# A recurrent-memory attention layer with a gated MLP on one core: everything but the AV products in 32-column TensorE tiles, both AV products side by side in shared accumulators, side work in one accumulator

## The chip, the core and the metric

The kernel runs on one core of a Trainium2 chip. The metric is the device time of one launch in microseconds. TensorE (PE; its weight loads are listed apart as PEld), VectorE (DVE), ScalarE (ACT), GpSimd (POOL) and SyncE (SP, which issues the DMAs here) each run their own instruction queue in order and meet at semaphores.

## What is computed

The reference, cut to what matters. S = 2048 tokens, Dm = 512, H = 32 heads of Dh = 128, M = 8 memory rows, segments of 32 tokens (64 of them).

```python
mem = mem0
for s in range(n_seg):
    h = concat([mem, x[s*32:(s+1)*32]])              # 40 rows
    q, k, v = h @ Wq, h @ Wk, h @ Wv                 # per head
    scores = where(mask, q @ k.T * scale, -1e9)
    p = softmax(scores)
    o = (p @ v) @ Wo
    mem = o[:8]                                      # goes into the next segment
    outs.append(o[8:])
a = concat(outs)
b = gelu(layernorm(x) @ w1 + b1) @ w2 + b2
g = sigmoid((x * gate_w).sum(-1))
out = g * a + (1 - g) * b
```

The memory rows make the 64 segments a strict recurrence: the first matmul of a segment needs the last result of the segment before.

## The kernel before

**Stages.** A first stage computes the MLP branch and the gate for all tokens, and ends at about 104.7 us. Then one Python loop, `for s in range(nseg + 2)`, unrolls the 64 segments; a *tile* is four segments (`T, si = divmod(s, 4)`, 128 tokens). The order of every engine's instructions is that of the program text (a manual schedule).

**Rows.** Of a segment's 40 rows, 32 (8 memory, 24 tokens) ride through the loop body in `hT`; the remaining 8 tokens of each of a tile's four segments, the "left" rows, are computed for a whole tile at once, one tile ahead, as side work.

**One segment, in the order of PE's queue.** (1) Q and K in five accumulators, four 32-column tiles side by side (`qk_unit`); each is transposed in 32x32 blocks by DVE from PSUM into an fp32 tile `Tt` (`qk_tr`) and cast to bf16 into `QT` or `KT` by ACT, one of them by POOL. (2) The first half of V, cast by ACT. (3) `scores`, added in PSUM bank 7 to a mask that `mask_mm` wrote there in the segment before; in between and after them the second half of V. (4) ACT's `Exp`, first over the 16 columns of the memory queries, then over the rest, into `E`. (5) `sm`, the sums for the memory queries: two matmuls with the block matrix `BO`; DVE's reciprocal `R`, and DVE's product `Pm`. (6) The AV product of the memory rows, `Um`, in 32-row tiles (`av`). (7) `sr`, the sums for the token queries, in bank 7, and DVE's reciprocal of them, 256 columns long. (8) DVE and ACT cast `Um` into `UTT`. (9) Wo in two halves of 256 columns (`wo_unit`) for the new memory rows and the token rows of two segments before; casts into `wsb`. (10) `mask_mm` for the next segment in bank 7. (11) The AV product of the token rows of segment s-1 (`av_x`), from `Px`, which POOL multiplied (`x_mul`) once the long reciprocal was there. (12) Four small matmuls of `wsb` with `Sel`, which write the transposed new memory into bank 7, and DVE's cast into the next `hT`. `ux_out`, at the head of the next segment, lets ACT cast the token rows' AV product into `UTT`.

**Side work.** `side_work(T, si)` is a generator; each `next` issues one unit, four matmuls of 512 columns side by side. For si = 0 it gives 8 units of V of the left rows (`left_v`), for si = 1 and 2 8 units of their Q and K (`left_qk`), for si = 3 2 units of `out_units` and 8 of `wo_left`. `run_fill(n)` places n units: 5 behind `sm` (6 for si = 3), 1 behind `sr`, 2 ahead of (12) for si = 3; what is left follows (12). Tiles 0 and 15 have no side units in some of their segments. A unit's accumulator comes from `side`, banks 5 and 6 in turn; its evictions wait in two lists, `dve_q` and `act_q`, which `flush` empties at fixed places, and earlier if `side` needs the bank.

**Left Q and K.** DVE transposes the accumulator as in (1) into `Tt`, and POOL casts from there into `QL` and `KL`.

**Banks.** Q, K, V and the AV products rotate through banks 0 to 4 (`ring`); 7 holds mask, scores, `sr` and the new memory in one tile, so that `mask_mm` waits for whoever read the last one there.

```python
            S_next = mask_mm()
        if live and s >= 1:
            av_x(s - 1, (ne, na, nc_, nb))
        run_fill(2 * (si == 3))
```

Of the kernel before, what the change touches and what calls it, by code (L numbers as in the profile page):

```python
# [23 lines left out]
def kernel(ctx, tc, A_x, A_mem0, A_Wq, A_Wk, A_Wv, A_Wo, A_seg_len, B_x, B_w1, B_b1, B_w2, B_b2, gate_w, out):  # L24
    nc = tc.nc
    P = 128
# [147 lines left out]

    pools.update(nTt=2, nside=1)

# [13 lines left out]
    def later(q, ev, k):  # L190
        side_todo.add(k)
        q.append((k, ev))

    def side(shape, dtype=FP32):
        side_n[0] += 1
        n = pools["nside"]
        while side_n[0] - n in side_todo:
            flush(dve_q)
            flush(act_q)
        return bank(5 + side_n[0] % n, shape, dtype)  # L200

# [51 lines left out]
    def left_qk(T, t, hf):  # L253
        h0, h1 = HF[hf]
        bk = side([P, 512])
        side_k = side_n[0]
        for kc in range(KC):
            qk_unit(bk, GLs[T], t, h0, h1, kc)
            if kc < KC - 1:
                yield  # L260
        def ev():
            Tv = qk_tr(bk, h0, h1)
            if t == 0:
                nc.gpsimd.tensor_copy(out=QL[T % 2][:, h0:h1, :], in_=Tv)
            else:
                for hh in range(h0 // 8, h1 // 8):
                    r0 = 8 * hh - h0
                    nc.gpsimd.tensor_copy(out=KL[T % 2][:, :, :, hh, :], in_=Tv[:, r0:r0 + 8, :].rearrange("p g (s c) -> p g s c", c=LEFT))
        later(dve_q, ev, side_k)
        yield  # L270

    def left_v(T, vb):
        bk = side([P, 512])
        side_k = side_n[0]
        for kc in range(KC):
            v_unit(bk, GLs[T], vb, kc)
            if kc < KC - 1:
                yield

        def ev():  # L280
            vt = pools["sb"].tile([P, 4, Dh], BF16, tag="vt", bufs=1, name="vt")
# [12 lines left out]

        later(act_q, ev, side_k)
        yield
# [19 lines left out]
    def out_units(T):  # L316
        ob = side([P, Dm])
        side_k = side_n[0]
# [8 lines left out]
        def ev():  # L327
            o_sb = cw.tile([P, Dm], BF16, tag="o", bufs=1, name="o")
            nc.vector.scalar_tensor_tensor(out=o_sb[:], in0=ob[:], scalar=g_all[:, T:T + 1], in1=c_all[:, T, :], op0=ALU.mult, op1=ALU.add)
            nc.sync.dma_start(out2[T * P:(T + 1) * P, :], o_sb[:])  # L330
        later(dve_q, ev, side_k)
        yield
# [19 lines left out]
    def prep_q(s):  # L352
        T, si = divmod(s, SPT)
        nc.gpsimd.tensor_copy(out=QT[:, :, 32:40], in_=QL[T % 2][:, :, LEFT * si:LEFT * si + LEFT])

    def mask_mm():

        B = bank(7, [P, 512])
        S = B[:, 0:NG * EW].rearrange("p (i e) -> p i e", e=EW)
        nc.tensor.matmul(S, lhsT=ident[:], rhs=MkA[:].unsqueeze(2).to_broadcast([P, 4, 2, EW]),  # L360
                         start=True, stop=True, skip_group_check=True)
        return B, S
# [14 lines left out]

    def av(U, n, s, V, Pt, c_main, c_left, u0):

        T, si = divmod(s, SPT)  # L380
        for i in range(NG):
            for j in range(4):
                q = slice(32 * j, 32 * j + 32)
                nc.tensor.matmul(U[j][:, i, :], lhsT=V[q, i, :], rhs=Pt[q, i, c_main:c_main + n],  # L384
                                 start=(i == 0), stop=False, skip_group_check=True, tile_position=(32 * j, 0))
        for g in range(2):
# [97 lines left out]
    def setup():  # L484
# [13 lines left out]
        for hf in range(2):  # L498
            for t in range(2):
                yield from left_qk(0, t, hf)  # L500
                flush(dve_q)
                yield
        left_v_in(0)
# [75 lines left out]
    cw = loop.enter_context(tc.tile_pool(name="cw", bufs=2))  # L579
    pools.update(ps=pb, sb=cw, nTt=3, nside=2)  # L580

# [24 lines left out]

    def av_x(s, banks):
        U = [bank(k, [P, NG, 32]) for k in banks]
        av(U, 32, s, Vs.pop(s), Pxs.pop(s), 0, 32, 24)
        Uxs[s] = U  # L610

    def ux_out(s):
        T, si = divmod(s, SPT)
        c0 = 24 - 8 * si
        for j, U in enumerate(Uxs.pop(s)):
            nc.scalar.copy(out=UTT[T % 2][:, :, j, c0 + M:c0 + 40], in_=U[:])  # L616

    for s in range(nseg + 2):
# [11 lines left out]
        if live:  # L630
            B, S = S_next
            na, nb, nc_, nd, ne = ring
            ring = (nd, ne, na, nc_, nb)
            qk_banks = (na, nb, nc_, nd, ne)
# [27 lines left out]
            for kc in range(1, KC):  # L662
# [6 lines left out]
            sm = bank(nc_, [P, NG, 8])  # L669
            nc.tensor.matmul(sm[:], lhsT=BO[:], rhs=E[:, :, 8:16], start=True, stop=False)  # L670
            nc.tensor.matmul(sm[:], lhsT=BO[:], rhs=E[:, :, 0:8], start=False, stop=True)  # L671
            nc.scalar.copy(out=v_out(V, 1), in_=vb1[:])
            run_fill(5 + (si == 3))
            nc.vector.reciprocal(out=R[:, 0:8 * NG].rearrange("p (i q) -> p i q", q=8), in_=sm[:])  # L674
            Pm = cw.tile([P, NG, 16], BF16, tag="Pm", bufs=1, name="Pm")
            nc.vector.tensor_tensor(out=Pm[:].rearrange("p i (a q) -> p i a q", q=8), in0=E[:, :, 0:16].rearrange("p i (a q) -> p i a q", q=8),  # L676
                                    in1=R[:, 0:8 * NG].rearrange("p (i q) -> p i q", q=8).unsqueeze(2).to_broadcast([P, NG, 2, 8]), op=ALU.mult)
            Um = [bank(k, [P, NG, 8]) for k in (nd, ne, na, nc_)]
            av(Um, 8, s, V, Pm, 8, 0, 0)
            sr = B[:, 0:NG * 32].rearrange("p (i q) -> p i q", q=32)  # L680
            nc.tensor.matmul(sr, lhsT=BO[:], rhs=E[:, :, 16:48], start=True, stop=False, skip_group_check=True)  # L681
            nc.tensor.matmul(sr[:, :, 24:32], lhsT=BO[:], rhs=E[:, :, 48:56], start=False, stop=True, skip_group_check=True)
            Tp, sp = divmod(s - 2, SPT)
            for j in range(4):
                (nc.scalar.copy if j % 2 else nc.vector.tensor_copy)(out=UTT[Tp % 2][:, :, j, 24 - 8 * sp:24 - 8 * sp + M], in_=Um[j][:])  # L685
            nc.vector.reciprocal(out=R[:, 8 * NG:].rearrange("p (i q) -> p i q", q=32), in_=sr)  # L686
            run_fill(1)
        else:
            if s == nseg:
                ux_out(s - 2)  # L690
                x_mul(s - 1)
                av_x(s - 1, (ne, na, nc_, 7))
            else:
                ux_out(s - 2)
# [3 lines left out]
        for half in range(2):  # L698
            d = slice(256 * half, 256 * half + 256)
            wp = bank((nb, nd)[half], [P, 256])  # L700
            for u in range(8):
                wo_unit(wp, UTT[Tp % 2], 24 - 8 * sp, u, 256 * half, 256 * half + 256)
            if half == 0:
                flush(act_q, 2)
            (nc.scalar.copy if half else nc.vector.tensor_copy)(out=wsb[:, d], in_=wp[:])  # L705
        if s >= 2:
            wsbs[s] = wsb
        if s + 1 < nseg:
            S_next = mask_mm()
        if live and s >= 1:  # L710
            av_x(s - 1, (ne, na, nc_, nb))
        run_fill(2 * (si == 3))
        if s + 1 < nseg:
            aT = S_next[0][:, NG * EW:NG * EW + KC * M].rearrange("p (k m) -> p k m", m=M)
            for m in range(KC):
                nc.tensor.matmul(aT[:, m, :], lhsT=wsb[:, m * P:(m + 1) * P], rhs=Sel[:, 0:M], start=False, stop=True, skip_group_check=True)  # L716
            nc.vector.tensor_copy(out=hn[:, :, 0:M], in_=aT)  # L717
# [3 lines left out]
    for _ in out_units(NT - 2):  # L721
        flush(dve_q, 9)
    for _ in wo_left(NT - 1):
# [138 lines left out]
```

## Time and profile before

| | us |
|---|---|
| median of 6 runs | 838.56 (838.32 to 839.36) |
| the profiled execution: its time | 839.98 |
| its span | 838.1 |
| PE busy | 809.0 (97%) |
| DVE busy | 502.5 (60%) |
| ACT busy | 434.3 (52%) |
| POOL busy | 274.6 (33%) |
| a segment with si = 0, 1, 2 / 3 (a tile from 509.78) | 11.00, 10.95, 11.04 / 11.66 |

The loop of 64 segments takes from 104.7 us to the end, and nearly all of them have the length of the last row, so a segment is the unit to think in: 0.1 us of a segment is about 6.4 us of the whole. A segment begins where PE starts the first matmul on the new `hT`.

In timelines a line is a group of like instructions that follow each other on one engine: start, time from the first one's start to the last one's end, engine, line of the kernel, operation, tiles. Matmuls are pipelined, so the end of one group lies behind the start of the next. The form `128*32` is a weight tile of 128 rows and 32 columns; `128*128` takes the whole array, `32*128` is a 32-row tile.

### The profile page before, as it was taken

The numbers are of one execution on the slowest core, as the hardware profiler recorded it, in microseconds if no ns is written. First come the engines' busy times: TensorE is split into PE (matmuls) and PEld (weight loads), VectorE is DVE, ScalarE is ACT, GpSimd is POOL, SyncE is SP. The second block draws the span as 40 slices with busy tenths as digits, with TensorE's granted clock in tenths as the row PEclk, the third lists the DMA queues.
The fourth block names the chain that finished last, engine by engine and source line by source line (L and its number), as shares of the span: only waits on it lengthen the run. The fifth ranks groups of instructions, "written<-read, shape, count | busy, mean of one in ns | idle before, by whom it ended". The sixth has DMA issues, their size and how long they took to land.

```text
span 838.1 us, 49253 instructions
## 1 busy us (share of the span) xinstructions
PE 809.0 (97%) x22417; PEld 494.0 (59%) x22417; DVE 502.5 (60%) x1019; ACT 434.3 (52%) x1245; POOL 274.6 (33%) x625
## 2 busy tenths in 40 slices
PE   6999999999999999999999999999999999999886
PEld 3665455666666556665665665666556656665553
DVE  5763156565656666665666565666666565656553
ACT  3554445545554555545555545455554555455552
POOL 8000134242433243243424242433333243424220
PEclk9999999999999999999999999999999999999999
DMA  9790300000000010101010100001010101010000
GB/s 312 262 384 26 102 26 13 25 15 15 25 19 27 10 36 10 36 11 34 5 31 15 30 17 21 25 18 28 10 36 10 36 10 36 4 35 6 10 5 23
DMA packets 38216, 37.64 MB, mean 45 GB/s; under 512 B 13545, under 2 KB 36434, under 8 KB 36466
## 3 DMA queue, kind: packets, MB, share of 16 engines
q1 hardware_dynamic: 37874, 34.31, 12.4%
q8 instruction: 177, 2.90, 1.5%
q14 instruction: 37, 0.30, 0.1%
q0 software_dynamic: 128, 0.13, 0.1%
HBM read 26.03 MB, written 6.29 MB: 39 GB/s over the span
## 4 chain that ended last, share of the span: by engine, by line
PE 93%; DVE 3%; DMA 1%; issue 1%; SPq 1%; ACT 1%; DVEq 0%; ACTq 0%
PE b L211 34%; PE b L233 17%; PE b L222 17%; PE b L384 5%; PE hp L456 4%; PE bp L473 4%; PE b L360 2%; PE b L369 2%; PE b L681 2%; PE b L716 1%; PE b L389 1%; PE b L670 1%; DMA Wo_sb<-in_A_x_dram 1%; PE b L320 1%; PE b L373 0%
## 5 line engine op out<-in xcount | busy, mean ns | idle before, releaser
L217 DVE STREAM_TRANSPOSE Tt<-b 128x512 f32<-128x512 f32 (+1 forms) x384 | 225.9, 614 | 86.9 <-PE b L211 72.7
L211 PEld LDWEIGHTS <-hT 128*32 128x32 bf16 x5120 | 134.7, 97 | 100.0 <-DVE hT L717 15.4
L233 PE MATMUL b<-Wo_sb,UTT 128*32 128x256 bf16 (+1 forms) x4736 | 162.7, 285 | 1.2 <-ACT UTT L616 0.8
L222 PE MATMUL b<-Wv_sb,hT 128*32 128x512 bf16 x2048 | 141.8, 378 | 0.0
L211 PE MATMUL b<-Wq_sb,hT 128*32 128x512 bf16 x2048 | 132.9, 379 | 1.4 <-DVE hT L717 1.4
L211 PE MATMUL b<-Wk_sb,hT 128*32 128x256 bf16 (+1 forms) x3072 | 133.4, 308 | 0.0
L233 PEld LDWEIGHTS <-UTT 128*32 128x32 bf16 x4736 | 121.3, 97 | 19.2 <-ACT UTT L616 1.5
L651 ACT CAST KT<-Tt 128x256 bf16<-128x256 f32 (+1 forms) x192 | 87.2, 476 | 53.8 <-DVE Tt L217 53.7
L602 POOL TENSOR_TENSOR Px<-E,R 128x256 bf16<-128x256 bf16 x64 | 43.1, 673 | 219.1 <-DVE R L686 219.1
L686 DVE RECIPROCAL R<-b 128x256 f32<-128x256 f32 x64 | 112.5, 1757 | 0.0
L651 POOL CAST QT<-Tt 128x512 bf16<-128x512 f32 x64 | 39.3, 614 | 193.5 <-DVE Tt L217 193.5
L616 ACT CAST UTT<-b 128x256 bf16<-128x256 f32 x256 | 76.8, 386 | 24.3 <-PE b L389 23.8
L705 ACT CAST wsb<-b 128x256 bf16<-128x256 f32 x66 | 24.6, 373 | 119.9 <-PE b L233 119.9
L674 DVE RECIPROCAL R<-b 128x64 f32<-128x64 f32 x64 | 35.6, 557 | 79.4 <-PE b L671 79.4
L651 ACT CAST QT<-Tt 128x512 bf16<-128x512 f32 x64 | 39.6, 619 | 67.0 <-DVE Tt L217 67.0
L384 PEld LDWEIGHTS <-V 32*128 32x128 bf16 x4096 | 35.1, 91 | 46.8 <-DVE Pm L676 32.3
L222 PEld LDWEIGHTS <-hT 128*32 128x32 bf16 x2048 | 49.5, 96 | 21.2
L461 ACT ACTIVATE hg<-hp,b_sb 128x256 bf16<-128x256 f32 x80 | 37.8, 474 | 44.3 <-PE hp L456 44.2
L685 ACT CAST UTT<-b 128x64 bf16<-128x64 f32 x128 | 20.9, 215 | 75.3 <-PE b L389 75.3
L456 PE MATMUL hp<-yT,w_sb 128*128 128x256 bf16 (+1 forms) x352 | 54.0, 278 | 3.0 <-ACT hg L461 1.5
L604 POOL TENSOR_TENSOR racc<-racc,R 128x320 f32<-128x320 f32 x64 | 55.6, 868 | 0.0
L717 DVE CAST hT<-b 128x32 bf16<-128x32 f32 x63 | 12.1, 192 | 63.0 <-PE b L716 63.0
(116 smaller groups left out, 1080.6 us busy)
## 6 DMA issues: line engine op xcount, KB each, us to landing
Wv_sb<-in_A_Wv_dram SPq DMA_DIRECT2D x4, 1024.0 KB
Wq_sb<-in_A_Wq_dram SPq DMA_DIRECT2D x4, 1024.0 KB
Wk_sb<-in_A_Wk_dram SPq DMA_DIRECT2D x4, 1024.0 KB
Wo_sb<-in_A_Wo_dram SPq DMA_DIRECT2D x2, 2048.0 KB
vd<-vt SPq DMA_DIRECT2D x32, 128.0 KB
vs<-vd SPq DMA_DIRECT2D x256, 16.0 KB
out_dram<-o SPq DMA_DIRECT2D x16, 128.0 KB
Wo_sb<-in_A_x_dram SPq DMA_DIRECT2D x1, 1024.0 KB
```

Source lines behind the costliest of these rows:

```text
L211: nc.tensor.matmul(bk[32 * j:32 * j + 32, 0:n], lhsT=G[:, kc, :], rhs=W5[t][:, kc, h0:h1, j, :], start=(kc == 0), stop=(kc == KC - 1), til ...
L217: nc.vector.transpose(out=Tt[:, 0:n], in_=bk[:, 0:n])
L222: nc.tensor.matmul(bk[32 * j:32 * j + 32, :], lhsT=G[:, kc, :], rhs=Wv5[:, kc, 4 * vb:4 * vb + 4, j, :], start=(kc == 0), stop=(kc == KC - ...
L233: nc.tensor.matmul(bk[32 * g:32 * g + 32, :], lhsT=ut[:, i, j, c0:c0 + 32], rhs=Wo_sb[:, 4 * i + j, d0:d1], start=(j == 0 and i < 4), stop ...
L384: nc.tensor.matmul(U[j][:, i, :], lhsT=V[q, i, :], rhs=Pt[q, i, c_main:c_main + n], start=(i == 0), stop=False, skip_group_check=True, til ...
L456: nc.tensor.matmul(hp[:rows, :], lhsT=w1_sb[:, kc, fc * P:fc * P + rows], rhs=yTs[blk][:, kc, :], start=(kc == 0), stop=(kc == KC - 1))
L461: nc.scalar.activation(out=hg_[:rows, :], in_=hp[:rows, :], func=ACTF.Gelu_apprx_tanh, bias=b1_sb[:rows, fc:fc + 1], scale=1.0)
L602: nc.gpsimd.tensor_tensor(out=Px[:, :, 0:32], in0=E[:, :, 16:48], in1=Rr, op=ALU.mult)
L604: nc.gpsimd.tensor_tensor(out=racc[:], in0=racc[:], in1=R[:], op=ALU.add)
L616: nc.scalar.copy(out=UTT[T % 2][:, :, j, c0 + M:c0 + 40], in_=U[:])
L651: (nc.gpsimd.tensor_copy if bi == 2 else nc.scalar.copy)(out=dst, in_=Tv)
L686: nc.vector.reciprocal(out=R[:, 8 * NG:].rearrange("p (i q) -> p i q", q=32), in_=sr)
```

## The change

- `sums` replaces the `sm` and `sr` matmuls, `mem_out` the four of step (12), and `mask_mm` is rewritten: each matmul of a 128-column weight becomes four of 32 columns, each for its own 32 output partitions. After that only `av` uses another tile form.
- Both AV products stand together: `av` for the token rows of s-1 is moved from behind `mask_mm` to just before `av` for the memory rows of s, in the same four accumulators `U4` (columns 64 to 319 and 0 to 63), so the second starts no new group. The order of the ring changes with it.
- Side units: 3 instead of 5 behind `sm` (5 instead of 6 for si = 3), 2 behind `mask_mm` in all segments.
- `side` has one bank (5); bank 6 goes to `out_units` and to Wo's second half.
- Left Q and K: ACT casts the accumulator into a bf16 tile `lt`, and DVE transposes that straight into `QL` or `KL`. POOL's casts are gone.
- `out_units` is evicted by ACT (times the gate) and POOL (plus `c_all`) in place of DVE, but for the last tile.
- `wsb`: ACT casts the first half and DVE the second, where it was the other way round.

```diff
     def side(shape, dtype=FP32):
         side_n[0] += 1
-        n = pools["nside"]
-        while side_n[0] - n in side_todo:
-            flush(dve_q)
+        while side_n[0] - 1 in side_todo:
             flush(act_q)
-        return bank(5 + side_n[0] % n, shape, dtype)
+        return bank(5, shape, dtype)
...
         def ev():
-            Tv = qk_tr(bk, h0, h1)
-            if t == 0:
-                nc.gpsimd.tensor_copy(out=QL[T % 2][:, h0:h1, :], in_=Tv)
-            else:
-                for hh in range(h0 // 8, h1 // 8):
-                    r0 = 8 * hh - h0
-                    nc.gpsimd.tensor_copy(out=KL[T % 2][:, :, :, hh, :], in_=Tv[:, r0:r0 + 8, :].rearrange("p g (s c) -> p g s c", c=LEFT))
-        later(dve_q, ev, side_k)
+            lt = pools["sb"].tile([P, 512], BF16, tag="lt", name="lt")
+            nc.scalar.copy(out=lt[:], in_=bk[:])
+
+            def tr():
+                if t == 0:
+                    nc.vector.transpose(out=QL[T % 2][:, h0:h1, :].rearrange("p h r -> p (h r)"), in_=lt[:])
+                else:
+                    for hh in range(h0 // 8, h1 // 8):
+                        r0 = 32 * (8 * hh - h0)
+                        nc.vector.transpose(out=KL[T % 2][:, :, :, hh, :],
+                                            in_=lt[:, r0:r0 + 256].rearrange("p (g s c) -> p g s c", s=SPT, c=LEFT))
+            dve_q.append((None, tr))
+        later(act_q, ev, side_k)
...
-        ob = side([P, Dm])
+        ob = bank(6, [P, Dm])
...
+        if T == NT - 1:
             nc.vector.scalar_tensor_tensor(out=o_sb[:], in0=ob[:], scalar=g_all[:, T:T + 1], in1=c_all[:, T, :], op0=ALU.mult, op1=ALU.add)
-            nc.sync.dma_start(out2[T * P:(T + 1) * P, :], o_sb[:])
-        later(dve_q, ev, side_k)
+        else:
+            of = cw.tile([P, Dm], FP32, tag="Tt", bufs=pools["nTt"], name="of")
+            nc.scalar.activation(out=of[:], in_=ob[:], func=ACTF.Copy, scale=g_all[:, T:T + 1])
+            nc.gpsimd.tensor_tensor(out=o_sb[:], in0=of[:], in1=c_all[:, T, :], op=ALU.add)
+        nc.sync.dma_start(out2[T * P:(T + 1) * P, :], o_sb[:])
...
+    def sums(o, rhs, start, stop):
+        for j in range(4):
+            q = slice(32 * j, 32 * j + 32)
+            nc.tensor.matmul(o[q], lhsT=BO[:, q], rhs=rhs, start=start, stop=stop, skip_group_check=True, tile_position=(0, 32 * j))
+
+    def mem_out(aT, wsb):
+        for m in range(KC):
+            for c in range(4):
+                nc.tensor.matmul(aT[32 * c:32 * c + 32, m, :], lhsT=wsb[:, m * P + 32 * c:m * P + 32 * c + 32], rhs=Sel[:, 0:M],
+                                 start=False, stop=True, skip_group_check=True, tile_position=(0, 32 * c))
+
     def mask_mm():
 
         B = bank(7, [P, 512])
         S = B[:, 0:NG * EW].rearrange("p (i e) -> p i e", e=EW)
-        nc.tensor.matmul(S, lhsT=ident[:], rhs=MkA[:].unsqueeze(2).to_broadcast([P, 4, 2, EW]),
-                         start=True, stop=True, skip_group_check=True)
+        for j in range(4):
+            q = slice(32 * j, 32 * j + 32)
+            nc.tensor.matmul(S[q], lhsT=ident[:, q], rhs=MkA[:].unsqueeze(2).to_broadcast([P, 4, 2, EW]),
+                             start=True, stop=True, skip_group_check=True, tile_position=(0, 32 * j))
...
-            ring = (nd, ne, na, nc_, nb)
+            ring = (nb, nd, ne, na, nc_)
...
-            nc.tensor.matmul(sm[:], lhsT=BO[:], rhs=E[:, :, 8:16], start=True, stop=False)
-            nc.tensor.matmul(sm[:], lhsT=BO[:], rhs=E[:, :, 0:8], start=False, stop=True)
+            sums(sm, E[:, :, 8:16], True, False)
+            sums(sm, E[:, :, 0:8], False, True)
             nc.scalar.copy(out=v_out(V, 1), in_=vb1[:])
-            run_fill(5 + (si == 3))
+            run_fill(3 + 2 * (si == 3) + (s == 0))
...
-            Um = [bank(k, [P, NG, 8]) for k in (nd, ne, na, nc_)]
-            av(Um, 8, s, V, Pm, 8, 0, 0)
+
+            U4 = [bank(k, [P, NG * 40]) for k in (nd, ne, na, nc_)]
+            Um = [u[:, 0:NG * 8].rearrange("p (i q) -> p i q", q=8) for u in U4]
+            Ux = [u[:, NG * 8:].rearrange("p (i q) -> p i q", q=32) for u in U4]
+            if s >= 1:
+                av(Ux, 32, s - 1, Vs.pop(s - 1), Pxs.pop(s - 1), 0, 32, 24)
+                Uxs[s - 1] = Ux
+            av(Um, 8, s, V, Pm, 8, 0, 0, first=(s == 0))
             sr = B[:, 0:NG * 32].rearrange("p (i q) -> p i q", q=32)
-            nc.tensor.matmul(sr, lhsT=BO[:], rhs=E[:, :, 16:48], start=True, stop=False, skip_group_check=True)
-            nc.tensor.matmul(sr[:, :, 24:32], lhsT=BO[:], rhs=E[:, :, 48:56], start=False, stop=True, skip_group_check=True)
+            sums(sr, E[:, :, 16:48], True, False)
+            sums(sr[:, :, 24:32], E[:, :, 48:56], False, True)
...
             run_fill(1)
+            flush(act_q, 2)
...
-            wp = bank((nb, nd)[half], [P, 256])
+            wp = bank((nb, 6)[half], [P, 256])
...
-            if half == 0:
-                flush(act_q, 2)
-            (nc.scalar.copy if half else nc.vector.tensor_copy)(out=wsb[:, d], in_=wp[:])
+            (nc.vector.tensor_copy if half else nc.scalar.copy)(out=wsb[:, d], in_=wp[:])
...
             S_next = mask_mm()
-        if live and s >= 1:
-            av_x(s - 1, (ne, na, nc_, nb))
-        run_fill(2 * (si == 3))
+        run_fill(2)
         if s + 1 < nseg:
             aT = S_next[0][:, NG * EW:NG * EW + KC * M].rearrange("p (k m) -> p k m", m=M)
-            for m in range(KC):
-                nc.tensor.matmul(aT[:, m, :], lhsT=wsb[:, m * P:(m + 1) * P], rhs=Sel[:, 0:M], start=False, stop=True, skip_group_check=True)
+            mem_out(aT, wsb)
```

More of the change, by code (lines that the diff above doesn't have):

```diff
@@ L173 @@
                                     fill=MASK_NEG, base=M, channel_multiplier=-1)
-    pools.update(nTt=2, nside=1)
+    pools["nTt"] = 2
     def bank(k, shape, dtype=FP32):
@@ L280, in ev @@
         def ev():
-            vt = pools["sb"].tile([P, 4, Dh], BF16, tag="vt", bufs=1, name="vt")
+            vt = pools["sb"].tile([P, 4, Dh], BF16, tag="lt", name="vt")
             nc.scalar.copy(out=vt[:].rearrange("p i e -> p (i e)"), in_=bk[:])
@@ L316, in out_units @@
     def out_units(T):
-        ob = side([P, Dm])
-        side_k = side_n[0]
+        ob = bank(6, [P, Dm])
         for si in range(SPT):
@@ L325, in out_units @@
                              tile_position=(0, 32 * si))
-        def ev():
-            o_sb = cw.tile([P, Dm], BF16, tag="o", bufs=1, name="o")
+        o_sb = cw.tile([P, Dm], BF16, tag="o", bufs=1, name="o")
+        if T == NT - 1:
             nc.vector.scalar_tensor_tensor(out=o_sb[:], in0=ob[:], scalar=g_all[:, T:T + 1], in1=c_all[:, T, :], op0=ALU.mult, op1=ALU.add)
-            nc.sync.dma_start(out2[T * P:(T + 1) * P, :], o_sb[:])
-        later(dve_q, ev, side_k)
+        else:
[3 more added lines that the diff above has]
+        nc.sync.dma_start(out2[T * P:(T + 1) * P, :], o_sb[:])
         yield
@@ L376, in scores, with av @@
                                  start=False, stop=True, skip_group_check=True, tile_position=(0, 32 * j))
-    def av(U, n, s, V, Pt, c_main, c_left, u0):
+    def av(U, n, s, V, Pt, c_main, c_left, u0, first=True):
         T, si = divmod(s, SPT)
@@ L384, in av @@
                 nc.tensor.matmul(U[j][:, i, :], lhsT=V[q, i, :], rhs=Pt[q, i, c_main:c_main + n],
-                                 start=(i == 0), stop=False, skip_group_check=True, tile_position=(32 * j, 0))
+                                 start=(first and i == 0), stop=False, skip_group_check=True, tile_position=(32 * j, 0))
         for g in range(2):
@@ L500, in setup @@
                 yield from left_qk(0, t, hf)
+                flush(act_q)
+                yield
                 flush(dve_q)
-                yield
         left_v_in(0)
@@ L579 @@
     cw = loop.enter_context(tc.tile_pool(name="cw", bufs=2))
-    pools.update(ps=pb, sb=cw, nTt=3, nside=2)
+    pools.update(ps=pb, sb=cw, nTt=3)
     man = tc.manual_schedule()
@@ L605, in x_mul @@
         Pxs[s] = Px
[L607 to L610, printed above, removed]
     def ux_out(s):
@@ L615, in ux_out @@
         for j, U in enumerate(Uxs.pop(s)):
-            nc.scalar.copy(out=UTT[T % 2][:, :, j, c0 + M:c0 + 40], in_=U[:])
+            nc.scalar.copy(out=UTT[T % 2][:, :, j, c0 + M:c0 + 40], in_=U)
     for s in range(nseg + 2):
@@ L677 @@
                                     in1=R[:, 0:8 * NG].rearrange("p (i q) -> p i q", q=8).unsqueeze(2).to_broadcast([P, NG, 2, 8]), op=ALU.mult)
-            Um = [bank(k, [P, NG, 8]) for k in (nd, ne, na, nc_)]
-            av(Um, 8, s, V, Pm, 8, 0, 0)
+            U4 = [bank(k, [P, NG * 40]) for k in (nd, ne, na, nc_)]
[5 more added lines that the diff above has]
+            av(Um, 8, s, V, Pm, 8, 0, 0, first=(s == 0))
             sr = B[:, 0:NG * 32].rearrange("p (i q) -> p i q", q=32)
-            nc.tensor.matmul(sr, lhsT=BO[:], rhs=E[:, :, 16:48], start=True, stop=False, skip_group_check=True)
-            nc.tensor.matmul(sr[:, :, 24:32], lhsT=BO[:], rhs=E[:, :, 48:56], start=False, stop=True, skip_group_check=True)
+            sums(sr, E[:, :, 16:48], True, False)
+            sums(sr[:, :, 24:32], E[:, :, 48:56], False, True)
             Tp, sp = divmod(s - 2, SPT)
             for j in range(4):
-                (nc.scalar.copy if j % 2 else nc.vector.tensor_copy)(out=UTT[Tp % 2][:, :, j, 24 - 8 * sp:24 - 8 * sp + M], in_=Um[j][:])
+                (nc.scalar.copy if j % 2 else nc.vector.tensor_copy)(out=UTT[Tp % 2][:, :, j, 24 - 8 * sp:24 - 8 * sp + M], in_=Um[j])
             nc.vector.reciprocal(out=R[:, 8 * NG:].rearrange("p (i q) -> p i q", q=32), in_=sr)
             run_fill(1)
+            flush(act_q, 2)
         else:
@@ L691 @@
                 x_mul(s - 1)
-                av_x(s - 1, (ne, na, nc_, 7))
+                Ux = [bank(k, [P, NG, 32]) for k in (nd, ne, na, nc_)]
+                av(Ux, 32, s - 1, Vs.pop(s - 1), Pxs.pop(s - 1), 0, 32, 24)
+                Uxs[s - 1] = Ux
             else:
@@ L721 @@
     for _ in out_units(NT - 2):
-        flush(dve_q, 9)
+        pass
     for _ in wo_left(NT - 1):
```

## The prediction

> **What bounds the kernel now.** I read the page's busy times and chain first, then PE's timeline of one ordinary segment, then one in which PE has no side work.
>
> ```profile
> PE 809.0 (97%) x22417; PEld 494.0 (59%) x22417; DVE 502.5 (60%) x1019; ACT 434.3 (52%) x1245; POOL 274.6 (33%) x625
> ...
> PE 93%; DVE 3%; DMA 1%; issue 1%; SPq 1%; ACT 1%; DVEq 0%; ACTq 0%
> ```
>
> PE is never idle by the page, and the chain is PE. But this does not say that PE streams all the time. The ordinary segment (si = 1, from 520.78):
>
> ```profile
> 525.61 0.82 PE L222 MATMUL b<-Wv_sb,hT 128*32 128x512 bf16 x12
> 526.36 0.20 PE L670 MATMUL b<-E,BO 128*128 128x64 bf16 x1
> 526.40 0.19 PE L671 MATMUL b<-E,BO 128*128 128x64 bf16 x1
> 526.52 1.05 PE L211 MATMUL b<-Wq_sb,GL 128*32 128x512 bf16 x16
> ...
> 527.72 0.36 PE L384 MATMUL b<-Pm,V 32*128 32x8 bf16 x32
> ...
> 528.56 1.92 PE L233 MATMUL b<-Wo_sb,UTT 128*32 128x256 bf16 x64
> 530.41 0.36 PE L360 MATMUL b<-MkA,ident 128*128 128x448 bf16 x1
> 530.71 0.37 PE L384 MATMUL b<-Px,V 32*128 32x32 bf16 x32
> ```
>
> Four 512-column matmuls side by side (a quad) take 0.216 us: a block of 16 in the QK part takes 0.86. Wo is 16 quads of 256 columns at 0.109, 1.74 us, but 528.56 to 530.41 is 1.85. Three V quads make 0.65, but 525.61 to 526.36 is 0.75. The mask needs 0.19 and takes 0.30; the second `sm` matmul needs 0.03 and takes 0.12. So every change of tile form costs about 0.10 us, and a segment has nine of them (before and after `sm`, before and after `Um`, behind `sr`, around the mask, behind the token AV, behind `mem_out`): 0.9 of 11 us.
>
> In tile 0 the segment with si = 3 has no side units, so the bare latencies of the recurrence show:
>
> ```profile
> 144.60 0.20 PE L670 MATMUL b<-E,BO 128*128 128x64 bf16 x1
> ...
> 145.88 0.36 PE L384 MATMUL b<-Pm,V 32*128 32x8 bf16 x32 [1.05 <-DVE Pm L676]
> ...
> 146.67 1.93 PE L233 MATMUL b<-Wo_sb,UTT 128*32 128x256 bf16 x64
> 146.67 1.76 DVE L686 RECIPROCAL R<-b 128x256 f32<-128x256 f32 x1
> ...
> 149.22 0.26 PE L716 MATMUL b<-Sel,wsb 128*128 128x8 bf16 x4
> ...
> 149.76 0.61 PE L211 MATMUL b<-Wq_sb,hT 128*32 128x512 bf16 x8 [0.29 <-DVE hT L717]
> ```
>
> `sm` to `Um` cannot be under 1.28 us (reciprocal, `Pm`), `Um` to Wo not under 0.79 (copies to `UTT`), `Um` to the end of the long reciprocal 2.55, and from `mem_out` to the next QK 0.54, or 0.45 from its last matmul. In the ordinary segment these four stand at 1.36, 0.84, 2.55 and 0.63: the drains removed can give back only what lies above them.
>
> [...] `Pm` takes 0.29 us, but 0.41 in the si = 2 segment from 531.73, where POOL's `VL` copy (1.04 us) runs into it. [...]
>
> **The change, part by part,** in us from a segment's first QK matmul.
>
> *QKV, scores, exp.* Unchanged for PE. It would reach `sm` at 5.48 without the drain, but `sm` needs the first Exp, whose accumulator read ends at 5.49 for si = 1 (526.08 + 0.20 - 520.78) and 5.55 otherwise. In the one segment where PE waited for it (from 486.83) it started 0.05 later. So `sm` starts at 5.54 (5.60) instead of 5.58 (5.63): the drain of 0.10 gives 0.04. The later value comes from Q's third transpose waiting for POOL's read of a `Tt` buffer. With the left transposes out of the `Tt` ring, that falls on the first transpose, which has slack, except for si = 0. I take 5.60 for si = 0 and 5.55 for the others.
>
> *`sm` to `Um`.* PE: two `sums` 0.05, 3 units 0.65, drain 0.10. The token AV would then start at 0.80; its fourth bank is that of `sm`, free 0.88 after its start (0.04 to the last `sums`, 0.23 to the reciprocal, 0.56 for it, 0.05 handover). With 0.28 for 40 matmuls it ends at 1.17. `Um` needs 1.28, so PE stalls 0.11 and the interval is 1.28. With si = 3 (5 units) it is 0.05 + 1.08 + 0.10 + 0.28 = 1.51, against 1.57 before.
>
> *`Um` to Wo.* PE: 0.27 to the last `Um` start, drain 0.11, `sr` 0.14, one unit 0.22: 0.73. `UTT` needs 0.79, which decides.
>
> *Wo to `mem_out`.* Wo now ends at 0.79 + 1.75 = 2.54 after `Um`. The mask overwrites bank 7, which the long reciprocal reads until 2.55; with 0.05 handover the mask starts at 2.60, a wait that had 0.09 to spare. Behind it in PE's queue are only the mask 0.19 and two units 0.43: `mem_out` at 3.22. The second half of `wsb` (Wo's end, 0.05, DVE 0.36, 0.05) is there at about 3.18, so it is just covered. Sixteen small matmuls at 7 ns (as in `scores`): last one at 3.33.
>
> *To the next QK.* 0.45, as bare; two units (0.43) cover it.
>
> Sum: si = 0: 5.60 + 1.28 + 3.33 + 0.45 = 10.66; si = 1 and 2: 10.61; si = 3: 5.55 + 1.51 + 3.78 = 10.84. Before: 11.00, 10.95, 11.04, 11.66. Gains 0.34, 0.34, 0.43, 0.82. For si = 3 it is largest, since before only one unit stood behind `mem_out`, and PE waited for `hT`.
>
> Fifteen tiles with side units: 15 x 1.11 = 16.7 for si = 0 to 2, 15 x 0.82 = 12.3 for si = 3. Tile 0's si = 3: 10.79 to 10.52, 0.3. Tile 15's si = 0 to 2: 0.9 together. The second segment loses 1.6 now to a side bank that comes late, and about 1.1 after: 0.5. Tail: the copies of the token AV start earlier (-0.4), `out_units` waits for bank 6 (+0.5): nothing. MLP stage: its side units keep their places: nothing. Sum 30.7.
>
> *Covered edits.* ACT's cast to `lt` (64 of 0.61, the `vt` row) would be 39 us of ACT, which is idle for 48%; its places decide. The first of a segment stands ahead of Wo's first `wsb` half in ACT's queue, which waits behind it: the unit ends at about 0.95 after `Um`, the cast 0.6 later, and the half is there only at 1.9 (0.79 + 0.82 + 0.27), so 0.3 is to spare; the next unit on bank 5 comes at 2.8. If it came later than that, `wsb` and then `mem_out` would move with it. The second stands at the next segment's head behind four copies of the token AV (1.2 us), which wait for Wo's end as they overwrite what Wo reads; it ends about 0.9 into the segment, and ACT's next work, the first cast into `QT`, comes at 1.85. `wsb` halves: ACT is free at half one, DVE from 2.55 on. Eviction of `out_units`: ACT 0.68 (the `c_all` row) ends before `UTT`; POOL about 1.4 (an estimate from the `racc` row, 868 ns for 320) ends 1 us before it gets `Px` to do. The DMA of the output sits in SP's queue behind POOL, and nothing urgent follows. POOL's 44 us of casts go, so the `VL` copy leaves `Pm` alone. Left transposes: I take 0.7 us; below nothing no, and above see D.
>
> The profiled execution: 839.98 - 30.7 = 809.3. Its own time is 1.4 above the median, which I correct for: 838.56 - 30.7, about **807.8**.
>
> **Rivals.**
> A, the sum above: 807.8, own range 802 to 813. Chance 0.63.
> B, the latencies hide less than I think and all seven drains come back: 64 x 0.70 = 45, plus about 5 for si = 3: 789. For it: nine drains are seen. Against it: the segment without side work. 0.06.
> C, PE is not fed. Four segments of before have a gap of 0.48 to 0.74 us between two matmuls with "issue" as cause, three of them inside an AV burst; the two AVs now stand together, 80 pairs in a row, and 27 matmuls are added per segment. If a gap of 0.6 came in every fourth segment: +10, 818. Against it: the stall ahead of `Um` lets the queue refill. 0.19.
> D, slower. The bf16 transposes into `KL` write runs of 8 elements. Two stand between the last K transpose and the `sm` reciprocal, in si = 2 and 3; DVE has 1.6 us there (525.00 to 526.63). Each microsecond beyond costs one in 30 segments. At 0.41 each (the fp32 row of 256 columns) nothing; the change loses from 1.3 each on; at 1.5 it is 30 x 1.4 = 42, 850. Nothing seen speaks for three times the fp32 price. 0.09.
> E, the gain goes into waits not seen, within 0.2%: 0.03.
>
> **Numbers.** A measurement tells 0.2%, 1.7 us, from no change. Faster: A, B, C, 0.88; same 0.03; slower 0.09. Range 799 to 820, A with C, leaving out B, D, E.
>
> **What would show it.** Right: no 0.10 at `sm`, mask and `mem_out`; PE waiting for `Pm` about 0.1 and for R at the mask; segments of 10.6 to 10.9. Wrong: DVE late at the `sm` reciprocal (D), "issue" gaps in AV (C), or PE waiting for ACT on bank 5.

## The result: the undisturbed segment is shorter, and PE waits for its own instructions

The changed kernel takes 841.13 us (839.28 to 844.03), the one before 838.56: ratio 1.0034, 95% interval 1.0027 to 1.004. The forecast was 807.8. The profiled execution took 840.43 us, its span is 838.6 (before: 839.98 and 838.1).

From the page of the changed kernel: busy times, PE by tenths, the instruction queue, the chain.

```profile
PE 796.7 (95%) x24133; PEld 512.0 (61%) x24133; DVE 500.7 (60%) x1036; ACT 479.2 (57%) x1324; POOL 247.8 (30%) x544
...
q8 instruction: 190, 3.11, 1.6%
...
PE 91%; issue 3%; DVE 2%; DMA 1%; SPq 1%; ACT 1%; POOL 0%; POOLq 0%; DVEq 0%; ACTq 0%
```

PE is busy 12 us less than before, in a span as long. The share of the chain under "issue", time in which an engine waits for nothing that the profile shows, went from 1% to 3%. The list of PE's waits (time in total, times, longest) says where:

```profile
PE b L232 <- issue: 10.5, 24, 0.8
...
PE b L365 <- issue: 2.4, 4, 0.7
```

L232 is Wo, L365 the sums. In the same list of the kernel before, Wo has no such wait; the longest two are those of the AVs and of Q and K:

```profile
PE b L384 <- issue: 1.0, 2, 0.6
...
PE b L211 <- issue: 0.4, 1, 0.4
```

These figures are counted from modelled ends; from start to start the gaps are longer.

First a segment in which none of this happens (si = 1, 10.70 us long; PE's timeline, with one line of DVE):

```profile
661.65 0.24 PE L365 MATMUL b<-E,BO 128*32 128x64 bf16 x8
661.71 0.83 PE L210 MATMUL b<-Wq_sb,GL 128*32 128x512 bf16 x12
662.47 0.43 PE L403 MATMUL b<-Px,V 32*128 32x32 bf16 x32
662.75 0.23 PE L408 MATMUL b<-Px,VL 32*128 32x32 bf16 x8
662.95 0.36 PE L403 MATMUL b<-Pm,V 32*128 32x8 bf16 x32
...
663.74 1.93 PE L232 MATMUL b<-Wo_sb,UTT 128*32 128x256 bf16 x64
663.77 1.76 DVE L707 RECIPROCAL R<-b 128x256 f32<-128x256 f32 x1
665.58 0.37 PE L379 MATMUL b<-MkA,ident 128*32 128x448 bf16 x4
665.77 0.62 PE L210 MATMUL b<-Wk_sb,GL 128*32 128x512 bf16 x8
666.20 0.27 PE L370 MATMUL b<-Sel,wsb 128*32 128x8 bf16 x16
666.30 0.61 PE L210 MATMUL b<-Wk_sb,GL 128*32 128x512 bf16 x8
```

No 0.10 stands at `sm` or `mem_out` any more, and the mask hands over to the next matmuls in 0.19. From Wo to the mask it is still 1.84 (1.85 before), now because the mask waits for the long reciprocal: it starts 0.05 us after the end of that (663.77 + 1.76). Then another segment with si = 1, 11.62 us long:

```profile
527.28 0.36 PE L403 MATMUL b<-Pm,V 32*128 32x8 bf16 x32
...
528.07 0.62 PE L232 MATMUL b<-Wo_sb,UTT 128*32 128x256 bf16 x15
529.42 1.59 PE L232 MATMUL b<-Wo_sb,UTT 128*32 128x256 bf16 x49 [0.73 <-issue]
530.74 0.46 PE L379 MATMUL b<-MkA,ident 128*32 128x448 bf16 x4
```

In the middle of Wo, whose data are all there, PE starts nothing for 1.0 us. If PE's records in the whole trace (matmuls, weight loads, a few semaphore instructions) are numbered in order of their starts, 36 gaps of over 0.4 us between two starts, all in the loop, have something in common: the number of the first record behind each is 193 plus a multiple of 256. After the first stage there are 25 more gaps of that length; no two of them share a residue, and most end a wait for data that the profile names. In the kernel before there are four at the residue 193. Queue q8 brings 190 packets of 16 KB, and 48,284 PE records are 188.6 times 256: by this count a packet is 256 instructions (of 64 bytes, an estimate from 16 KB and 256), and the gaps stand where one packet's instructions end. The queue's packets against these gaps, from the trace of the changed kernel:

```
packet starts   lands     PE goes on   after landing
526.36          528.04    529.42       1.38
538.57          539.68    541.20       1.52
617.54          618.71    620.25       1.54
```

Over all 36 it is 1.39 us from landing to PE's next start, with a standard deviation of 0.12.

To separate the two effects I take the shortest segment of each si in tiles 1 to 14 as undisturbed, and add up what the 63 intervals between segment starts have above it ("stalls" below; not all of it is supply).

| | si = 0 / 1 / 2 / 3, undisturbed | their sum | loop | stalls |
|---|---|---|---|---|
| before | 11.00 / 10.94 / 11.03 / 11.66 | 44.64 | 706.8 | 4.3 |
| changed | 10.72 / 10.70 / 10.78 / 11.01 | 43.22 | 707.5 | 27.0 |

Without stalls the loop went from 702.5 to 680.4 us, 22 us less; the stalls took 23 back.

### The profile page after: what moved, and what is told of

Same layout as the page of the kernel before. It is cut to its first block, busy times and chain, and to the rows that moved or that the text cites. A ratio compares the mean times of both kernels' runs of the same rounds, so it can differ in the third digit from the quotient of the medians.

```text
span 838.6 us, 52738 instructions
## 1 busy us (share of the span) xinstructions
PE 796.7 (95%) x24133; PEld 512.0 (61%) x24133; DVE 500.7 (60%) x1036; ACT 479.2 (57%) x1324; POOL 247.8 (30%) x544
## 4 chain that ended last, share of the span: by engine, by line
PE 91%; issue 3%; DVE 2%; DMA 1%; SPq 1%; ACT 1%; POOL 0%; POOLq 0%; DVEq 0%; ACTq 0%
PE b L210 33%; PE b L232 18%; PE b L221 16%; PE b L403 5%; PE hp L475 4%; PE bp L492 4%; PE b L365 3%; PE b L379 2%; PE b L388 2%; PE b L370 1%; PE b L408 1%; DMA Wo_sb<-in_A_x_dram 1%; PE b L392 0%; DVE Tt L216 0%; PE b L323 0%
## 5 line engine op out<-in xcount | busy, mean ns | idle before, releaser
L216 DVE STREAM_TRANSPOSE Tt<-b 128x512 f32<-128x512 f32 (+1 forms) x320 | 180.9, 595 | 76.9 <-PE b L210 63.6
L232 PE MATMUL b<-Wo_sb,UTT 128*32 128x256 bf16 (+1 forms) x4736 | 171.8, 285 | 11.0 <-issue 10.5
L232 PEld LDWEIGHTS <-UTT 128*32 128x32 bf16 x4736 | 123.1, 96 | 37.8 <-issue 18.8
L210 PE MATMUL b<-Wq_sb,hT 128*32 128x512 bf16 x2048 | 134.8, 380 | 1.7 <-DVE hT L736 1.6
L403 PEld LDWEIGHTS <-V 32*128 32x128 bf16 x4096 | 43.7, 91 | 33.0 <-issue 28.2
L262 ACT CAST lt<-b 128x512 bf16<-128x512 f32 x64 | 37.5, 586 | 31.9 <-PE b L210 13.6
L727 ACT CAST wsb<-b 128x256 bf16<-128x256 f32 x66 | 24.6, 373 | 46.1 <-PE b L232 46.1
```

What stands on the lines that cost most here:

```text
L210: nc.tensor.matmul(bk[32 * j:32 * j + 32, 0:n], lhsT=G[:, kc, :], rhs=W5[t][:, kc, h0:h1, j, :], start=(kc == 0), stop=(kc == KC - 1), til ...
L216: nc.vector.transpose(out=Tt[:, 0:n], in_=bk[:, 0:n])
L232: nc.tensor.matmul(bk[32 * g:32 * g + 32, :], lhsT=ut[:, i, j, c0:c0 + 32], rhs=Wo_sb[:, 4 * i + j, d0:d1], start=(j == 0 and i < 4), stop ...
```

## The experiments

Theory F, in its later form F2: instructions reach PE in blocks of 256, one in some 3.5 to 3.7 us, and PE stalls when it uses a block up faster. R1: only the two AVs side by side matter, however they are fed. R2: `wsb` and `mem_out` are late anyway. R3: it is the switches of the tile form (the prediction's "drains": 0.10 us each in the kernel before; what PE does in them is not shown). Gaps are counted from here on as above, over 0.4 us at a block's end, in the one traced execution of each kernel.

**`feed`: the supply by itself.** Ten stretches of 512 independent matmuls in 32-column tiles:

```diff
+    for n in WIDTHS:
+        for q in range(QUADS):
+            for j in range(4):
+                nc.tensor.matmul(acc[32 * j:32 * j + 32, 0:n], lhsT=x[:, 32 * j:32 * j + 32], rhs=w[:, 0:n], ...
```

> No part of the reference is computed: ten stretches of 512 independent matmuls (1,024 PE instructions with the weight loads) in 32-column tiles, of 16, 64, 128, 192, 256, 320, 384, 448, 512 and again 64 columns. F: the stretches up to about 256 columns all take the same time, some 14 to 15 us (3.6 to 3.8 us for each block of 256 instructions), with gaps every 256 instructions; from 320 on the time follows the columns (17 us at 320, 27.6 us at 512). Rival: the time follows the columns all the way down, 3.5 us at 64 and 7 us at 128, since fetches run ahead.

PE's timeline:

```profile
3.69 1.99 PE L33 MATMUL acc<-w,x 128*32 128x16 bf16 x223 [3.69 <-DMA x<-in_A_x_dram]
7.79 1.20 PE L33 MATMUL acc<-w,x 128*32 128x16 bf16 x128 [2.11 <-issue]
11.24 1.20 PE L33 MATMUL acc<-w,x 128*32 128x16 bf16 x128 [2.25 <-issue]
...
18.98 1.90 PE L33 MATMUL acc<-w,x 128*32 128x64 bf16 x128 [2.30 <-issue]
22.43 1.90 PE L33 MATMUL acc<-w,x 128*32 128x64 bf16 x128 [1.56 <-issue]
26.16 1.90 PE L33 MATMUL acc<-w,x 128*32 128x64 bf16 x128 [1.83 <-issue]
...
36.52 1.97 PE L33 MATMUL acc<-w,x 128*32 128x128 bf16 x128 [0.87 <-issue]
...
50.61 2.83 PE L33 MATMUL acc<-w,x 128*32 128x192 bf16 x128 [0.63 <-issue]
54.34 2.82 PE L33 MATMUL acc<-w,x 128*32 128x192 bf16 x128 [0.90 <-issue]
57.79 3.46 PE L33 MATMUL acc<-w,x 128*32 128x192 bf16 x128 [0.63 <-issue]
61.52 103.94 PE L33 MATMUL acc<-w,x 128*32 128x256 bf16 x2688 [0.26 <-issue]
```

128 matmuls with their loads are one block; the first 223 ran without a gap, so less than two blocks were in hand at the start. Blocks start every 3.45 or 3.73 us (once 4.01) whether they hold 16 or 192 columns a matmul; from 7.79 to 61.52, 15 blocks, the mean is 3.58. In the 256-column stretch (3.49 us of columns for a block) the gaps fade to 0.3 us, and beyond it there are none: F's forecast held. The period can be seen whole: PE goes on at 7.79, the next packet starts 1.12 us later (8.91), lands at 9.87, and PE goes on at 11.24. PE was through with the block it had (7.79 + 1.20) before the next packet landed: in this unbroken dense stretch nothing lay in reserve.

In the traces of the two kernels packets of q8 start at least 3.27 us apart (before; 3.31 changed). But where PE was slower the packets ran ahead of it. In the changed kernel one block took 3.94 us (from 546.22); PE entered the next at 550.16 and had used it up at 552.45, 2.29 us later and without a gap: the packet for the one behind it had started at 550.14, not 1.12 us behind the entry. Ahead of the gap at 529.42 it had started 0.66 us behind the entry (525.70) and was under way for 1.68.

That makes the density readable from the timelines. Before, from `sm` to Wo (526.36 to 528.56) there are 68 matmuls with their loads, 136 instructions in 2.20 us: 256 in 4.1 us. In the changed kernel (661.65 to 663.74) it is 224 in 2.09 us: 256 in 2.4, and Wo follows with 128 in 1.84, 256 in 3.7. The QK part has 160 in 3.5 us, 256 in 5.6.

**`b_split`: more instructions in the slow part, before the change.**

```diff
-                    qk_unit(bk, hc, t, h0, h1, kc)
+                    qk_unit(bk, hc, t, h0, h1, kc, 2 if bi < 2 else 1)
```

> The kernel before with the matmuls of the first Q and the first K accumulator split into two of 256 columns: 32 matmuls, 64 PE instructions more per segment, the same columns, nothing else. F: about 745 instructions per segment of 11 us, so gaps with issue as cause as in the changed kernel: 843 to 863 us. Rival (the count does not matter as long as PE's columns are the same): 838 to 840 and at most a handful of such gaps.

840.51 us, ratio 1.0032 (1.0021 to 1.0043), three gaps, stalls 3.5. My forecast for F (843 to 863) was wrong: as many instructions as in the changed kernel made no gaps here. The count alone isn't it; hence F2.

**`a_split`: the same edit on the changed kernel.**

> The changed kernel with the first Q and the first K accumulator of a segment in matmuls of 256 columns, as in b_split: 64 PE instructions more per segment (about 800), the columns, the dense stretch and all waits unchanged. F2: the supply of 256 instructions per 3.53 us gives at least 11.0 us for a segment, and the reserve that the slow QK part builds up is smaller: more and longer gaps, 850 to 880 us. Rival R1 (only the dense stretch matters; in b_split the same edit cost 2.4 us): 841 to 846.

850.38 us, 1.0164 (1.0139 to 1.0189). PE's waits:

```profile
PE b L234 <- issue: 12.1, 23, 0.9
...
PE b L367 <- issue: 2.7, 5, 0.8
PE b L405 <- issue: 2.5, 4, 1.0
```

43 gaps, and they reach into the AVs (L405). The same 64 instructions cost 2 us where the stretch behind is loose and 9 where it is dense. R1 had 841 to 846 and falls: the AVs stand as before, and yet the edit made more gaps.

**`b_tiling`: the 32-column tiling alone.** `sums`, `mem_out` and the new `mask_mm` in the kernel before; the AVs stay apart.

```diff
-            nc.tensor.matmul(sm[:], lhsT=BO[:], rhs=E[:, :, 8:16], start=True, stop=False)
-            nc.tensor.matmul(sm[:], lhsT=BO[:], rhs=E[:, :, 0:8], start=False, stop=True)
+            sums(sm, E[:, :, 8:16], True, False)
+            sums(sm, E[:, :, 0:8], False, True)
...
-                nc.tensor.matmul(aT[:, m, :], lhsT=wsb[:, m * P:(m + 1) * P], rhs=Sel[:, 0:M], start=False, stop=True, skip_group_check=True)
+            mem_out(aT, wsb)
```

> The kernel before with sm, sr, mask and mem_out in 32-column tiles and nothing else of the change: 54 PE instructions more per segment, the AVs apart. A pure count theory (as many instructions, as many gaps): about 30 gaps, 838 to 850 us. F2 and R1: the token AV stands behind the mask, so no stretch is as dense; at most ten gaps, and about five of the nine drains go, of which those at sm and mem_out show: 822 to 834 us.

838.70 us, 1.0005 (0.9995 to 1.0015): no difference. Undisturbed 10.87 / 10.82 / 11.00 / 11.43, stalls 8.4, eight gaps:

```profile
PE b L397 <- issue: 1.5, 4, 0.4
...
PE b L402 <- issue: 1.2, 5, 0.5
```

So the expected 4 to 16 us did not show; the time lies in the range of the pure count theory, but not its 30 gaps. The traced execution is the fastest of 13 (836.13), and in it the account closes: 8 us of shorter segments (0.52 in four, 15.75 times), 4 of them paid back in stalls, a span 3.7 below that of before. What costs the median execution 2.6 us more, no trace shows.

**`a_wide`: the rest of the change without the tiling.** `sm`, `sr`, mask and `mem_out` as before, everything else as changed.

> The changed kernel with sm, sr, mask and mem_out all as 128-column matmuls again: only the AVs' place, the side bank, the casts and the fills are as changed; 674 to 690 PE instructions per segment, as before the change. F2: about a third of the gaps stay (the two AVs still stand together), the drains around sr and mask come back on the path: 822 to 836 us. R1: the gaps stay as they are, and with drains 845 to 860.

844.32 us, 1.0081 (1.0067 to 1.0095). Undisturbed 11.03 / 11.01 / 11.01 / 11.44, sum 44.49 against 44.64 before: the rest of the change, the AVs' place among it, shortens next to nothing as long as the switches stay. Eight gaps, stalls 10.4, at the instruction count of before. My forecast had counted on a gain from the AVs' place that is not there. R1 (845 to 860) was near in time, but its gaps, as many as in the changed kernel, are not there either.

**`a_wo1` and `b_wo1`: fewer instructions at the same columns.** Wo in one accumulator, 64 instructions fewer:

```diff
-        for half in range(2):
-            d = slice(256 * half, 256 * half + 256)
-            wp = bank((nb, 6)[half], [P, 256])
-            for u in range(8):
-                wo_unit(wp, UTT[Tp % 2], 24 - 8 * sp, u, 256 * half, 256 * half + 256)
-            (nc.vector.tensor_copy if half else nc.scalar.copy)(out=wsb[:, d], in_=wp[:])
+        wp = bank(nb, [P, Dm])
+        for u in range(8):
+            wo_unit(wp, UTT[Tp % 2], 24 - 8 * sp, u)
+        for half in range(2):
+            d = slice(256 * half, 256 * half + 256)
+            (nc.vector.tensor_copy if half else nc.scalar.copy)(out=wsb[:, d], in_=wp[:, d])
```

> The changed kernel with Wo in one accumulator of 512 columns instead of two halves: 32 matmuls fewer per segment, so 64 PE instructions fewer (about 670 instead of 735), the columns streamed and every other edit unchanged; both casts into wsb follow Wo's end, side by side on ACT and DVE. Theory F (PE runs out of instructions, which reach it in blocks of 256): the gaps inside Wo and sr, about 35 of 0.5 to 1.1 us, go or become few, and the time falls to about 815 us (810 to 822). Rival R1 (the gaps come from the dense stretch of the two AVs, not from the count): the stretch is unchanged, so most gaps stay and the time is 832 to 841. Rival R2 (the change gains nothing because wsb and mem_out are late anyway): with the first half's cast later too, 841 to 860.

> The kernel before with the same single 512-column Wo. F: it has only four gaps with issue as cause (2.4 us in all), so 836 to 839 us. Rival (fewer weight loads and matmuls are worth time by themselves, whatever the supply): the same 20 to 25 us as in the changed kernel, about 815.

843.78 us (1.0066, 1.0053 to 1.008) and 849.21 (1.0129, 1.0113 to 1.0144): F missed both times, and the first lies in R2's range. In `a_wo1` the stalls fell from 27.0 to 11.6, but the undisturbed segments are all 0.22 to 0.31 longer. Its timeline shows why:

```profile
533.60 0.37 ACT L727 CAST wsb<-b 128x256 bf16<-128x256 f32 x1 [1.16 <-PE b L232]
...
534.00 0.42 DVE L727 CAST wsb<-b 128x256 bf16<-128x256 f32 x1 [0.58 <-ACT wsb L727]
...
534.48 0.21 PE L370 MATMUL b<-Sel,wsb 128*32 128x8 bf16 x8 [0.17 <-DVE wsb L727]
```

DVE's cast does not start beside ACT's but waits for its end: I had counted on both at once. Why is not shown: the two read one bank, and the casts into `UTT`, which write one tile from different banks, do run side by side (in the kernel before DVE's two run from 403.73 and ACT's two from 403.76). In `b_wo1` ACT waits for DVE in the same way. R2 does not explain it: in the changed kernel PE waits for `wsb` before `mem_out` only four times, 1.0 us in all (`PE b L370 <- DVE wsb L727: 1.0, 4, 0.3`). The stalls of `b_wo1` fell from 4.3 to 0.9. From Wo's first matmul to the mask it is 1.83 us there with 32 matmuls, 1.85 before with 64, so by themselves fewer matmuls are worth 0.02 us a segment, about 1 us in all.

**`a_wo1_act`: the same without that flaw.**

```diff
+        nc.scalar.copy(out=wsb[:], in_=wp[:])
```

> The changed kernel with Wo in one 512-column accumulator as in a_wo1, but cast into wsb by ACT alone in one piece, since the two casts from one bank stood one after the other there (mem_out 0.41 us late in 63 segments, 26 us). ACT's cast of 512 columns takes 0.59 us against 0.42 for DVE's half: F2: few gaps, mem_out 0.10 to 0.17 us later than in the changed kernel, so 838.6 - 26 (the gaps) + 6 to 11, 820 to 829 us. Rival (in a_wo1 the time went up because something besides the casts is lost with the second bank): 838 or more.

832.47 us, 0.9926 (0.9913 to 0.9938). PE's waits, and Wo in a segment without a gap:

```profile
PE b L365 <- issue: 2.1, 4, 1.0
...
PE b L232 <- issue: 1.1, 3, 0.4
```

```profile
556.13 1.91 PE L232 MATMUL b<-Wo_sb,UTT 128*32 128x512 bf16 x32
557.97 0.37 PE L379 MATMUL b<-MkA,ident 128*32 128x448 bf16 x4
```

Twelve gaps, stalls 11.7; undisturbed 10.82 / 10.82 / 10.82 / 11.12, 0.04 to 0.12 longer than in the changed kernel for ACT's longer cast (585 ns for 512 columns, where DVE's half took 425 there). 8.7 us below the changed kernel, with one edit that removes no column and lengthens the path. From Wo to the mask it is 1.84 us as in the changed kernel, where the long reciprocal sets it, so nothing is gained there: the gain is supply. It is 3 us short of what I expected because a third of the gaps stayed.

**`a_sm_mo`, `a_wo1_sm_mo`, `a_best`: buying instructions with switches.** `sm` and `mem_out` back in 128 columns, on the changed kernel and on `a_wo1_act`; `a_best` also has `run_fill(3 + (si == 3) + (s == 0))` and `run_fill(2 + (si == 3))`.

> The changed kernel with sm (2) and mem_out (4) as 128-column matmuls again: 36 PE instructions fewer per segment, about 700. Theory F2 (a stall comes when PE uses up a block of 256 instructions in less than the 3.5 to 3.7 us in which the next one arrives, so both the count and the dense stretch from the scores to the end of Wo matter): fewer and shorter gaps, and the four tile switches that come back lie beside DVE's work for Pm, the wait for wsb and the last units: 818 to 832 us. Rival R1 (only the adjacent AVs matter): gaps as before, 836 to 846. Rival R3 (the switches cost what they cost in the kernel before, 0.10 us each): 850 to 865.

> The changed kernel with Wo in one accumulator cast by ACT alone (a_wo1_act), and sm and mem_out as 128-column matmuls: 100 PE instructions fewer per segment than the change, about 630. F2: what lies above the undisturbed segment length falls from the 12 us of a_wo1_act to 5 or less, and the switches that come back lie beside DVE's work and the wait for ACT's cast: 823 to 829 us. Rival R3 (the drains show): 833 to 845.

> As a_wo1_sm_mo, and for si = 3 one side unit moved from behind sm to behind the mask, where PE waits for ACT's cast of wsb: 2 to 3 us less than a_wo1_sm_mo (0.15 to 0.2 us in 15 segments), 820 to 827 us. Rival (the unit is missed behind sm): no less than a_wo1_sm_mo.

841.54 (1.0042, 1.0029 to 1.0055), 833.46 (0.9939, 0.9926 to 0.9953) and 832.79 (0.9924, 0.9911 to 0.9938). The stalls fell each time, 27.0 to 18.2 and 11.7 to 8.1, but the undisturbed sum of four rose from 43.22 to 43.82 and from 43.59 to 43.83: the switches that I thought hidden cost 9 and 4 us. All three forecasts missed. The first time lies in R1's range, but with 24 gaps in place of 36; the second at the lower edge of R3's. R3 was right that the switches cost something, but at about 0.04 us each, not 0.10 (0.60 for 16 of them in `a_sm_mo`). Moving one unit in `a_best` gave 0.02 us in a segment with si = 3, not 0.15.

**`b_tiling_wo1`: few instructions and a loose stretch.** `b_tiling` with Wo in one accumulator (bank `nd`), cast by ACT alone.

> The kernel before with only the 32-column tiling (b_tiling) and Wo in one accumulator cast by ACT alone: about 670 PE instructions per segment, the AVs apart. F2: b_tiling's undisturbed segments are 0.13 us shorter on average than those of before (8 us in all), and its gaps (8 us) go: 829 to 833 us. Rival (b_tiling gained nothing because the drains are not on the path): 837 to 840. Rival (ACT's longer cast is late here too): 836 or more.

830.00 us, 0.9899 (0.9884 to 0.9914), inside the forecast: faster than both kernels, and the fastest one here. No gap at a block's end is over 0.4 us; undisturbed 10.89 / 10.83 / 11.02 / 11.25, 10 us less in the loop than before, and stalls 4.5, as before. Its chain:

```profile
PE 92%; DVE 4%; DMA 1%; issue 1%; SPq 1%; ACT 1%; DVEq 0%; ACTq 0%
```

With it the runs give count and density apart (gaps; "together" has the rest of the change with it):

| PE instructions per segment (si = 0 to 2) | AVs apart | AVs together |
|---|---|---|
| 664 | 0 (`b_tiling_wo1`) | 12 (`a_wo1_act`) |
| 728 | 8 (`b_tiling`) | 36 (changed) |
| 792 | | 43 (`a_split`) |

Each row down and each step to the right adds gaps: both theories that named one of the two alone were too narrow. (With sums, mask and `mem_out` in 128 columns, at 674, there are four in the kernel before and eight in `a_wide`. `b_split`, at 738, has three: what it adds stands in the slow part.)

## Why the prediction was wrong

**What held.** The latencies of the recurrence were right, step by step, in the segment shown (us; forecast in brackets): `sm` at 5.54 (5.55); `sm` to `Um` 1.30 (1.28); `Um` to Wo 0.79 (0.79); `Um` to the mask 2.63 (2.60), so PE does wait for the long reciprocal; `Um` to the last `mem_out` matmul 3.35 (3.33). From there to the next QK it is 0.51 (0.45), and 0.48 to 0.51 in the shortest segments of each si. With si = 3, `Um` to Wo is 0.85 (0.79) too. Sum 10.70 (10.61), and 11.01 (10.84) for si = 3. These small errors make 43.22 for the four instead of 42.72, 8 us of the whole: with them alone the kernel would have come out near 816.

**What failed.** The sum took it that PE gets an instruction whenever its data are there. Rival C named the stall, its cause ("PE is not fed") and the two edits behind it, but priced it with 0.6 us in every fourth segment, +10 us, at a chance of 0.19. The trace has 36 gaps in 64 segments, 0.70 us each on average and up to 1.12 (25.3 us in all), against 2.3 us before; of what lies above the undisturbed length 22.7 us are new. The term was too small by more than half, and it should have been in the sum. Latencies and stalls together close the account: the profiled execution, forecast at 809.3, took 840.43, 31.1 more, of which the latencies are 7.9 and the stalls 22.7. Two signs were in the profile of before: its four gaps stand multiples of 256 instructions apart, and q8 brings those 256 in a packet. My 10.6 us segments of 728 instructions would have asked for one packet per 3.73 us (728 / 256 = 2.84 of them), hardly more than the 3.58 that a block took on average in `feed`, with parts of the segment at 2.4. Those 3.58 came only with `feed`.

**The argument against C was wrong.** I wrote that the stall ahead of `Um` lets the queue refill. Packets did get ahead where PE was slower (the one at 550.14, above), but that stall is 0.1 us, and a block took 3.58 us in `feed`.

**The other rivals and covered edits.** D fell: the bf16 transposes into `KL` take 403 ns, those into `QL` 702 (0.41 and 0.7 taken; in the kernel before, 512 columns of fp32 from PSUM took 716, and there was no bf16 transpose to read). ACT's cast into `lt` takes 0.59 (0.61). E's number was nearest to the result, but for two large effects that cancel, not for a small gain.

**Open.** The changed kernel's times spread over 4.8 us, those of before over 2.3. That gaps vary with each packet's arrival would explain it, but no run here tests that, and `b_tiling`, with eight gaps in its trace, spreads over 4.7. Nor do I know why the unit moved in `a_best` gained nothing.

## What to carry to other kernels

Count instructions as well as columns. In `feed` a chain of short matmuls took 3.58 us on average for 256 instructions (128 matmuls with their loads), however few their columns; in the changed kernel, with parts at 256 in 2.4 us, a tiling that quarters a matmul to save a 0.10 us switch spent what it saved (22 us of shorter segments, 23 of stalls). A single block was faster where what stood before it was slow (2.29 us at 550.16). The sign was a gap under "issue" whose instruction number has a fixed residue modulo 256 (193, 36 times). What helped was fewer, wider matmuls in the dense stretch (8.7 us less in `a_wo1_act`), and the AVs apart (no gap in `b_tiling_wo1` against 12 in `a_wo1_act`, which has the rest of the change too).

## What the runs showed of the hardware

- In the traces of the two kernels packets of PE's instruction queue start at least 3.27 us apart. In `feed` a block of 256 PE instructions (matmuls and weight loads alike) came every 3.45 or 3.73 us (once 4.01) as long as it held 16 to 192 columns a matmul. Of the 3.45 us from 7.79, 1.12 went by until its packet started, 0.96 while it was under way, and 1.37 from landing to PE's next start. In the changed kernel a packet was under way for 0.9 to 1.7, and at the 36 gaps it was 1.19 to 1.60 from landing to PE's next start.
- In `feed`, matmuls of 16 to 192 columns in 32-column tiles took 28 ns each on average (3.58 us for 128), once they ran for more than a block.
- Instructions added where PE was slow (256 in 5.6 us) cost little: `b_split` adds 64 to each segment for 2 us. The same 64 cost 9 us in `a_split`. And a dense block behind a slow one passed without a gap in 2.29 us (changed kernel, 550.16).
